# Top-k attention and a highway layer on one core: score tiles kept for the whole run, last rows' first products tied to one top-eight, and fewer unread products behind a layer's

## The chip, the cores and the metric

The kernel runs on one core of a Trainium2 chip. The metric is the device time in microseconds (us) of one execution; the time before is the median of three runs. The engines are named as the profile names them: PE is TensorE (PEld its weight loads), DVE is VectorE, ACT is ScalarE, POOL is GpSimd, SP is SyncE, which issues most of the DMAs.

## The reference

Eight batch elements, eight heads, 576 rows, head size 64. Each row of the scores keeps its 32 largest values; the rest is masked before the softmax. The heads' outputs of a row are joined to 512 features, and a highway layer follows.

```python
scores = scale * np.matmul(q, k.transpose(0, 1, 3, 2))          # (8, 8, 576, 576)
kth = np.partition(scores, -top_k, axis=-1)[..., -top_k:-top_k + 1]   # top_k = 32
scores = np.where(scores >= kth, scores, -1000000000.0)
attn = softmax(scores)                                          # exp(s - max), over its sum
x = np.matmul(attn, v), heads side by side                      # (4608, 512)
H = np.maximum(x @ w_h, 0.0)
T = 1.0 / (1.0 + np.exp(-(x @ w_t + b_t)))
out = T * H + (1.0 - T) * x
```

## The kernel before

**Items.** A unit is 128 query rows of one head, or, for the last 64 rows (576 = 4 x 128 + 64), the last rows of two heads one above the other. Two units make a pair, here called an item; `pairs` has 144, 18 for each batch element: 16 of full rows and, at the end, 2 of last rows. The scores of an item fill three banks of PSUM (512 columns each): unit 0 in bank 0 and the first 64 columns of bank 1, unit 1 in the last 64 columns of bank 1 and all of bank 2. Two such score tiles exist (pool `xps`, `bufs=2`), so the scores of item g can be written only when all is done with those of item g - 2.

**The top 32 of a row** are not sorted out in full. VectorE takes the top eight of each of six 96-column segments (`segments`, L358, twelve a step), and from these 48 `refine` finds the row's largest value and a threshold near rank 24 (L375 to L391). ScalarE turns the scores into a mask of what lies above the threshold and counts it (`mask_count`, L406, twice a step). TensorE adds the mask, at a large negative weight, onto the scores in PSUM (`mask_add`, L419), and VectorE takes the top eight of what is left in each unit's full row (`below`, L432, twice a step). From the count and these eight the 32nd value is picked (L438, L448, L451). Exponents (L424), a mask by the 32nd value (L454, L457) and their minimum (L471, L474) make the weights, which SP's transposing DMA turns (L496) for the product with v (L509, three steps later). ScalarE copies finished outputs out of PSUM (L523).

**The order.** The program is written out by hand: `step(i)` issues, for every engine, what belongs to items i + 2 (scores), i + 1 (segments, threshold, mask), i (mask products, full top-eight, exponents), i - 1 (weights) and i - 3 (product with v). Each engine runs its own list in this order; semaphores join them. On TensorE a step is: the mask products of item i (L419), the products with v of item i - 3 (L509), eight unread products (`spare`, L279; three where the items coming are of last rows and the output tile is begun anew), at times a piece of the preparation for the next batch element (transposes of q and k, L251 and L258), the scores of item i + 2, then a piece of preparation or a layer's products if there is one (L537 to L551), and again unread products: four behind such a piece, ten where there is none.

```python
        if i + 2 < NG:
            start_scores(i + 2)
        if layers and (last_steps or i <= SPB or kind[0] or not to_prep):
            ...
            late.append(layers.pop(0)())
        ...
        spare(4 if late else 10)
```

`spare(n)` issues n products of 252 columns into columns of the output tile that nobody reads. The scores of full-row items are L311 and L322, those of last rows L328 (two heads one after the other, four products each) and L339 (the last 64 columns). The layer's inputs are turned by another DMA (L602), and its products wait for it. `finish` handles the last item and the last blocks.

Of the kernel before, what the change touches and what calls it, by code (L numbers as in the profile page):

```python
# [11 lines left out]
FP32 = mybir.dt.float32  # L12
# [14 lines left out]
def kernel(  # L27
# [10 lines left out]
    nc = tc.nc  # L38
    P = nc.NUM_PARTITIONS
# [13 lines left out]
    BANK = 512  # L53
# [13 lines left out]
    pairs = [(u, u + 1) for u in range(0, NU, 2)]  # L67
# [10 lines left out]
    xpool = ctx.enter_context(tc.tile_pool(name="x", bufs=3))  # L78
    fpool = ctx.enter_context(tc.tile_pool(name="f", bufs=2))
    hpool = ctx.enter_context(tc.tile_pool(name="h", bufs=3))  # L80
    xps = ctx.enter_context(tc.tile_pool(name="xps", bufs=2, space=bass.MemoryType.PSUM))
    ops = ctx.enter_context(tc.tile_pool(name="ops", bufs=1, space=bass.MemoryType.PSUM))
    fps = ctx.enter_context(tc.tile_pool(name="fps", bufs=1, space=bass.MemoryType.PSUM))


    ident_f = consts.tile([P, P], FP32)
# [12 lines left out]
    TOP, THR, KTH = 0, 1, NPK + 1  # L99
    wall = consts.tile([P, NU + 2, NPK + 2], FP32)  # L100
# [174 lines left out]
    def spare(n):  # L275
        if "t" not in po:
            po.update(t=pso_tile(), n=0)
        for _ in range(n):
            nc.tensor.matmul(  # L279
                po["t"][:, 4 * DE : BANK],  # L280
                ident_b[:],
                cst[:, 0 : BANK - 4 * DE],
                start=True,
                stop=True,
                skip_group_check=True,
            )

    def prep_alloc(kd):
        kT = kqpool.tile([P, NP, MAIN], FP32, name="kT")
        qT = kqpool.tile([P, NP, S], FP32, name="qT")  # L290
        return kT, qT, kd
# [2 lines left out]

    def scores(pair, prep):
        kT, qT, kd = prep
        ps = xps.tile([P, 3 * BANK], FP32, tag="x", name="xs")
        heads2 = [units[u][2] for u in pair]  # L300
        qt = units[pair[0]][1]
        qs = qt * P
        MB = 2 * BANK
        rest = []
        RA, RB = BANK, 2 * BANK - rem
        if qt < nfull:
            hp = heads2[0][0] // 2
            for n0 in range(0, MAIN, 256):
                for s, mo in ((0, 0), (1, MB)):
                    r = s * D  # L310
                    mm = nc.tensor.matmul(  # L311
                        ps[:, mo + n0 : mo + n0 + 256],
                        qT[r : r + D, hp, qs : qs + P],
                        kT[r : r + D, hp, n0 : n0 + 256],
                        start=(n0 == 0),
                        stop=True,
                        skip_group_check=True,
                    )
                    if s:
                        rest.append(mm)  # L320
            ends = ps[:, BANK:MB].rearrange("p (a n) -> p a n", n=rem)[:, 0 :: BANK // rem - 1, :]
            rest.append(nc.tensor.matmul(ends, qT[:, hp, qs : qs + P], kd[:, hp, :], start=True, stop=True))  # L322
        else:
            for (mo, ro), hh in zip(((0, RA), (MB, RB)), heads2):
                hp = hh[0] // 2
                for n0 in range(0, MAIN, 256):
                    for r in (0, D):
                        mm = nc.tensor.matmul(  # L328
                            ps[r : r + rem, mo + n0 : mo + n0 + 256],
                            qT[r : r + D, hp, qs : qs + rem],  # L330
                            kT[r : r + D, hp, n0 : n0 + 256],
                            start=(n0 == 0),
                            stop=True,
                            skip_group_check=True,
                        )
                        if mo:
                            rest.append(mm)
                for r in (0, D):
                    mm = nc.tensor.matmul(  # L339
                        ps[r : r + rem, ro : ro + rem],  # L340
                        qT[r : r + D, hp, qs : qs + rem],
                        kd[r : r + D, hp, r : r + rem],
                        start=(mo == 0),
                        stop=True,
                        skip_group_check=True,
                    )
                    rest.append(mm)
        both = bass.AP(tensor=ps.tensor, offset=ps[:].offset, ap=[ps[:].ap[0], [3 * BANK - S, 2], [1, S]])
        return ps[:, 0:S], ps[:, 3 * BANK - S : 3 * BANK], both, rest
# [49 lines left out]
    def biases(g):  # L399
        return nc.gpsimd.tensor_tensor(be[:, g], wall[:, 2 * g : 2 * g + 2, TOP : KTH + 1 : KTH - TOP], fac[:], ALU.mult)  # L400
# [22 lines left out]
    def expo(u, sc, e):  # L423
        nc.scalar.activation(e, sc, AF.Exp, bias=tb(u), scale=scale)  # L424
        return e
# [3 lines left out]
        return [t[:, s, :] for s in range(2)] + [t]  # L429

    def below(u, ps):
        nc.vector.max(wall[:, u, THR + 1 : KTH], ps)  # L432


    def hits(pair):
# [83 lines left out]
    def pso_tile():  # L519
        return ops.tile([P, BANK], FP32, tag="po", name="pso")  # L520
# [192 lines left out]
    preps = {0: prep_alloc(kds[0])}  # L713
# [4 lines left out]
    st = {}  # L718
# [4 lines left out]
    def ensure_prep(b, hp):  # L723
        for it in ((b, hp, 0), (b, hp, 1), (b, 0, 7), (b, 0, 8)):
            if it not in done:
                done.add(it)
                prep_piece(stages[b], preps[b], *it[1:])()
# [10 lines left out]
    def start_scores(g):  # L738
        b = units[pairs[g][0]][0]
        for u in pairs[g]:  # L740
            for h in units[u][2]:
                ensure_prep(b, h // 2)
        st[g] = dict(ps=scores(pairs[g], preps[b]), sc=[None, None], et=[None, None], e=[None, None])
        st[g]["seg"] = 0
        st[g]["cand"] = cands[g % len(cands)]

    def copy_both(g):
        st[g]["sc"] = copy_scores(st[g]["ps"][2])


    def segs(g, n):
        if g >= NG:
            return
        for c in range(st[g]["seg"], min(2 * NSEG, st[g]["seg"] + n)):
            s, k = divmod(c, NSEG)
            segments(st[g]["cand"][:, s], st[g]["ps"][s], k, k + 1, () if s else st[g]["ps"][3])
        st[g]["seg"] += n
# [24 lines left out]
    late = []  # L782
    kind = [False]

    def masks_of(g):
        pr = pairs[g]
        views = (st[g]["ps"][0], st[g]["sc"][1])
        st[g]["m"] = [mask_count(u, views[s]) for s, u in enumerate(pr)]

    def step(i):  # L790
# [5 lines left out]
        b, k_in = divmod(i, SPB)  # L796
# [15 lines left out]
        if live:  # L812
            pr = pairs[i]
# [18 lines left out]
        segs(i + 1, 2 * NSEG)  # L832
        if live:
            below(pr[0], st[i]["ps"][0])
            below(pr[1], st[i]["ps"][1])
        if live:
            st[i]["e"] = pair_tile("e")
            expo(pr[0], st[i]["sc"][0], st[i]["e"][0])
# [9 lines left out]
        elif i > SPB:  # L848
            kind[0] = True
            piece = prep_filler()  # L850
            if piece:
                late.append(piece)
        spare(4 if late else 10)
        if live:
            expo(pr[1], st[i]["sc"][1], st[i]["e"][1])
        ra = refine(i + 1, st[i + 1]["cand"]) if nxt else iter(())
# [53 lines left out]
    def begin():  # L910
        done.update((0, hp, part) for hp in range(NP) for part in range(2))
        done.update(((0, 0, 7), (0, 0, 8)))
        piece = partial(prep_piece, stages[0], preps[0])
        dve = nc.vector.tensor_copy
        spare(21)
        xa = xps.tile([P, 3 * BANK], FP32, tag="x", name="xs")
        ev0 = piece(0, 3)
        ev1 = piece(0, 5, xa, dve)
        ev2 = piece(0, 4, po["t"], dve)
        ev1()  # L920
        ev0()
        ev2()
        piece(0, 2, xa[:, BANK : 2 * BANK], dve)()
        po.clear()
        start_scores(0)
        piece(0, 6, pso_tile())()
        evs = [piece(1, 0), piece(1, 5, pso_tile())]
        for ev in evs:
            ev()
        segs(0, 2 * NSEG)  # L930
        copy_both(0)
        start_scores(1)
        for _ in refine(0, st[0]["cand"]):
            pass
        biases(0)
        evs = [piece(2, 0), piece(2, 5, pso_tile())]
        masks_of(0)
        for ev in evs:
            ev()
        rest = [(0, 3, 0), (0, 3, 1), (0, 1, 6), (0, 2, 6)]  # L940
        done.difference_update(rest)
        to_prep.extend(rest)
        vs = loads_v(0, vbs[0])
        todo_v.extend(vs[H:] + vs[0:H] + loads_w() + [load_bt])
# [20 lines left out]
    def finish():  # L965
        i = NG - 1
        pr, pu = pairs[i], pairs[i - 1]
# [39 lines left out]
        cur["e"] = pair_tile("e")  # L1007
        for s, u in enumerate(pr):
            expo(u, cur["sc"][s], cur["e"][s])
        x1 = xps.tile([P, 3 * BANK], FP32, tag="x", name="xs")  # L1010
        project(bank(x1, 1), z["qt"], z["xT"], wt, True)
        blk_gate(z, bank(x1, 1))
        n = values_of(i - 2, 2 * DE)
# [4 lines left out]
        old["et"] = transposes(pu[0])  # L1018
        nc.vector.tensor_tensor(hit[:], hit[:], wall[:, pr[0] : pr[1] + 1, THR:KTH], ALU.mult)
        pick_b(pr, hit)  # L1020
        x2 = xps.tile([P, 3 * BANK], FP32, tag="x", name="xs")
        cur["et"] = halves(et_tile())
        turned = None
        for s, home in enumerate((bank(x2, 1), bank(x1, 0))):
# [47 lines left out]
    with tc.If(fine < 1):  # L1072
        with tc.For_i(0, B, 1) as bi:
# [21 lines left out]
            prep = prep_alloc(kds[0])  # L1095
# [4 lines left out]
            for pr in pairs[0 : NG // B]:  # L1100
                scs = copy_scores(scores(pr, prep)[2])
                for s, u in enumerate(pr):
                    b, qt, heads = units[u]
                    if heads[0] == 0:
                        xs = xpool.tile([P, H * DE], FP32, name="xs")
                    sc = scs[s]
# [10 lines left out]
                    e = pair_tile("e")[s]  # L1117
# [45 lines left out]
```

## Time and profile before

| what | value |
|---|---|
| median of 3 runs | 797.43 us (797.13 to 797.91) |
| the profiled execution | 797.43 us, its span 795.7 us |
| VectorE busy | 767.3 us (96%) |
| ScalarE busy | 756.3 us (95%) |
| TensorE busy | 693.0 us (87%) |
| GpSimd busy | 564.8 us (71%) |
| granted TensorE clock, mean | 0.996 |

The span is the time from the first instruction to the last in the profiled execution. A row of the groups by line names line, engine, operation and tiles, then the count, the busy time, the mean of one in ns, and the idle time of the engine just before them with what ended it. A row of the timeline has start and length in us and, in brackets, idle time before it. A row of the list of waits has the total, the number of waits and the longest. In a row of busy time by stretch the engines stand in the order PE, PEld, DVE, ACT, POOL, behind them the granted clock, the share of the DMA engines and GB/s.

### The profile page before, as it was taken

What the parts mean: (1) busy time and instruction counts of PE and PEld (TensorE: products, weight loads), DVE (VectorE), ACT (ScalarE), POOL (GpSimd) and SP (SyncE); (2) the same over time, 40 slices, a digit from 0 to 9 for tenths busy, and PEclk for the clock granted to TensorE, in tenths of its full rate; (3) what the DMA queues carried; (4) which work ended last, traced back from release to release, by engine and by line L of the source; (5) the groups of instructions that cost most, each with busy time, mean ns of one, the idle gap of its engine ahead of it and who ended that gap; (6) DMA issues with size and microseconds to landing.
All of it is one profiled execution on the core that took longest, in us unless ns stands there. A gap on an engine that the chain in (4) does not pass through costs nothing.

```text
span 795.7 us, 20350 instructions
## 1 busy us (share of the span) xinstructions
PE 693.0 (87%) x6459; PEld 494.6 (62%) x6459; DVE 767.3 (96%) x3947; ACT 756.3 (95%) x1401; POOL 564.8 (71%) x750
## 2 busy tenths in 40 slices
PE   8889988888988888888997889888998888988884
PEld 6666766566656666566665666656666666666552
DVE  6999999999999999999999999999999999999996
ACT  5999999999999999999999999999999999999984
POOL 2666867877778767787777876788777787776760
PEclk9999999999999999999999999999999999999998
DMA  6699967976899567987689866898677975565643
GB/s 125 88 136 172 127 125 140 159 127 87 140 157 156 104 99 135 159 136 117 106 146 159 133 110 111 154 154 127 107 129 146 162 118 96 97 113 98 114 85 89
DMA packets 341780, 100.32 MB, mean 126 GB/s; under 512 B 326048, under 2 KB 333856, under 8 KB 341664
## 3 DMA queue, kind: packets, MB, share of 16 engines
q1 hardware_dynamic: 286448, 79.14, 52.6%
q0 software_dynamic: 53536, 19.34, 22.5%
q8 instruction: 53, 0.87, 0.4%
q10 hardware_dynamic: 1680, 0.46, 0.3%
q14 instruction: 63, 0.52, 0.2%
HBM read 31.72 MB, written 9.44 MB: 52 GB/s over the span
## 4 chain that ended last, share of the span: by engine, by line
DVE 46%; ACT 32%; PE 16%; issue 2%; DMA 2%; SPq 0%; POOL 0%; DVEq 0%; ACTq 0%; POOLq 0%
DVE cand L358 16%; DVE wall L432 15%; ACT m L406 9%; ACT e L424 8%; ACT sc L353 6%; DVE ep L471 6%; ACT r L454 4%; PE xs L328 4%; PE fp L537 3%; PE pso L279 3%; PE xs L419 2%; PE xs L311 2%; DMA xT<-xb 2%; ACT xs L523 2%; DVE en L382 1%
## 5 line engine op out<-in xcount | busy, mean ns | idle before, releaser
L358 DVE MAX8 cand<-xs 128x8 f32<-128x96 f32 x1728 | 298.0, 252 | 0.4 <-PE xs L311 0.2
L279 PE MATMUL pso<-cst,ident_b 128*128 128x252 bf16 x1841 | 247.1, 272 | 41.8 <-ACT xs L523 39.7
L457 POOL TENSOR_SCALAR r<-sc,wall 128x576 bf16<-128x576 f32 x135 | 232.5, 1722 | 0.0
L424 ACT ACTIVATE e<-sc,be 128x576 bf16<-128x576 f32 x288 | 227.8, 791 | 0.1
L279 PEld LDWEIGHTS <-ident_b 128*128 128x128 bf16 x1841 | 173.5, 98 | 80.7 <-issue 48.9
L432 DVE MAX8 wall<-xs 128x8 f32<-128x576 f32 x288 | 205.2, 756 | 13.3 <-PE xs L419 12.1
L311 PE MATMUL xs<-kT,qT 64*128 64x256 f32 x1024 | 145.3, 400 | 34.0 <-DVE high L375 26.0
L353 ACT COPY sc<-xs 128x1152 f32<-128x1152 f32 x144 | 161.7, 1123 | 0.2
L311 PEld LDWEIGHTS xs<-kT,qT 64*128 64x128 f32 x1024 | 93.0, 186 | 65.5 <-issue 39.3
L406 ACT ACTIVATE m<-xs,wall 128x576 int8<-128x576 f32 x144 | 108.1, 751 | 9.8 <-DVE wall L391 8.6
L471 DVE TENSOR_TENSOR ep<-e,r 128x1024 bf16<-128x1024 bf16 (+2 forms) x236 | 116.4, 493 | 0.3 <-issue 0.2
L448 POOL TENSOR_TENSOR hit<-hit,wall 128x18 f32<-128x18 f32 x143 | 32.1, 225 | 113.5 <-DVE hit L438 113.5
L419 PE MATMUL xs<-m,ident_b 128*128 128x512 bf16 (+1 forms) x576 | 104.7, 285 | 9.0 <-ACT m L406 6.8
L406 ACT ACTIVATE m<-sc,wall 128x576 int8<-128x576 f32 x144 | 112.5, 781 | 0.0
L454 ACT ACTIVATE r<-sc,be 128x576 bf16<-128x576 f32 x143 | 111.0, 776 | 0.0
L509 PEld LDWEIGHTS <-et 128*128 128x128 bf16 (+1 forms) x1600 | 68.6, 100 | 19.9 <-issue 3.5
L400 POOL TENSOR_TENSOR be<-wall,fac 128x4 f32<-128x4 f32 x144 | 29.0, 201 | 71.9 <-DVE ep L471 52.0
L509 PE MATMUL pso<-vb,et 128*128 128x65 bf16 (+1 forms) x1600 | 74.4, 194 | 1.0 <-DMA et<-ep 1.0
L419 PEld LDWEIGHTS <-ident_b 128*128 128x128 bf16 x576 | 51.1, 98 | 35.5 <-issue 13.9
L322 PEld LDWEIGHTS xs<-kd,qT 128*128 128x128 f32 x256 | 38.1, 188 | 42.5 <-issue 42.1
L322 PE MATMUL xs<-kd,qT 128*128 128x128 f32 x256 | 62.5, 326 | 0.0
L625 POOL TENSOR_TENSOR s<-h,x 128x512 f32<-128x512 f32 (+1 forms) x37 | 42.8, 1157 | 1.0 <-ACT h L624 1.0
(128 smaller groups left out, 1005.8 us busy)
## 6 DMA issues: line engine op xcount, KB each, us to landing
kin<-in_k_dram SPq DMA_DIRECT2D x64, 128.0 KB, 3.2
qin<-in_q_dram SPq DMA_DIRECT2D x62, 128.0 KB, 3.1
out_dram<-s SPq DMA_DIRECT2D x30, 256.0 KB, 3.1
s<-h POOLq DMA_DIRECT2D x29, 256.0 KB, 3.8
xb<-x POOLq DMA_DIRECT2D x30, 128.0 KB, 2.7
vb<-in_v_dram POOLq DMA_DIRECT2D x28, 128.0 KB, 3.9
et<-ep SPq DMA_TRANSPOSE x143, 3.9
vb<-in_v_dram POOLq DMA_DIRECT2D x24, 64.0 KB, 3.0
```

The costliest lines, as they stand in the source:

```text
L279: nc.tensor.matmul(po["t"][:, 4 * DE : BANK], ident_b[:], cst[:, 0 : BANK - 4 * DE], start=True, stop=True, skip_group_check=True,)
L311: mm = nc.tensor.matmul(ps[:, mo + n0 : mo + n0 + 256], qT[r : r + D, hp, qs : qs + P], kT[r : r + D, hp, n0 : n0 + 256], start=(n0 == 0), ...
L353: nc.scalar.copy(sc[:], both)
L358: ins = nc.vector.max(cand[:, s, :], sc[:, s * SEG : (s + 1) * SEG])
L406: nc.scalar.activation(m1[:].bitcast(I8)[:, 1 : 2 * S : 2], ps, AF.Sign, bias=wall[:, u, THR : THR + 1], scale=ABOVE, accum_out=csum[:, u ...
L419: nc.tensor.matmul(ps[:, s0:s1], ident_b[:], m1[:, s0:s1], start=False, stop=True, skip_group_check=True)
L424: nc.scalar.activation(e, sc, AF.Exp, bias=tb(u), scale=scale)
L432: nc.vector.max(wall[:, u, THR + 1 : KTH], ps)
L454: nc.scalar.activation(r, sc, AF.Relu, bias=eb(u), scale=BIGK)
L457: nc.gpsimd.tensor_scalar(r, sc, kth(u), None, ALU.is_ge)
L471: return nc.vector.tensor_tensor(out[:, :, c0:c1], e[:, :, c0:c1], r[:, :, c0:c1], ALU.min)
L509: nc.tensor.matmul(pso[r0 : r0 + ql, col : col + DE], ets[s][:, c, gi * P2 : gi * P2 + ql], vb[:, h, vc, :], start=(c == 0), stop=(c == nc ...
```

## The change

Three edits go together. First, the two score tiles are made once and kept for the run (`xss`), item g using tile g % 2; before, each item took a new tile from a pool of two. Second, the first four products of a last-row item (the ones into bank 0) are declared independent of the second full top-eight (unit 1's) of item g - 2, so that they wait for that item's first full top-eight only; `below` returns its instruction for this. Third, `spare(4 if late else 10)` becomes `spare(1 if late else 10)`: one unread product, not four, behind a layer's products or a piece of preparation. In the changed program's order of instructions there are 1481 unread products where there were 1841; the first L339 product of 16 last-row items has a wait on VectorE that it had not; and the first score product of 80 items no longer waits for TensorE's own signal beside another engine's.

```diff
-    xps = ctx.enter_context(tc.tile_pool(name="xps", bufs=2, space=bass.MemoryType.PSUM))
+    xps = ctx.enter_context(tc.tile_pool(name="xps", bufs=1, space=bass.MemoryType.PSUM))
...
+    xss = [xps.tile([P, 3 * BANK], FP32, name=f"xs{i}") for i in range(2)]
...
-    def scores(pair, prep):
+    def scores(pair, prep, other=None):
+        def ahead(mm):
+            if other is not None:
+                tc.declare_no_dep(mm.ins, other.ins, reason="another bank")
+
         kT, qT, kd = prep
-        ps = xps.tile([P, 3 * BANK], FP32, tag="x", name="xs")
+        ps = xss[pair[0] // 2 % 2]
...
                         if mo:
                             rest.append(mm)
+                        else:
+                            ahead(mm)
...
     def below(u, ps):
-        nc.vector.max(wall[:, u, THR + 1 : KTH], ps)
+        return nc.vector.max(wall[:, u, THR + 1 : KTH], ps)
...
-        st[g] = dict(ps=scores(pairs[g], preps[b]), sc=[None, None], et=[None, None], e=[None, None])
+        st[g] = dict(ps=scores(pairs[g], preps[b], st[g - 2]["below"] if g > 1 else None), sc=[None, None], et=[None, None], e=[None, None])
...
             below(pr[0], st[i]["ps"][0])
-            below(pr[1], st[i]["ps"][1])
+            st[i]["below"] = below(pr[1], st[i]["ps"][1])
...
-        spare(4 if late else 10)
+        spare(1 if late else 10)
...
-        xa = xps.tile([P, 3 * BANK], FP32, tag="x", name="xs")
+        xa = xss[1]
...
-        x1 = xps.tile([P, 3 * BANK], FP32, tag="x", name="xs")
+        x1 = xss[i % 2 ^ 1]
...
-        x2 = xps.tile([P, 3 * BANK], FP32, tag="x", name="xs")
+        x2 = xss[i % 2]
```

## The prediction

> **What bounds the kernel now.** I read the page first, for who is busy and what ends the waits of the busiest engine.
>
> ```profile
> PE 693.0 (87%) x6459; PEld 494.6 (62%) x6459; DVE 767.3 (96%) x3947; ACT 756.3 (95%) x1401; POOL 564.8 (71%) x750
> L279 PE MATMUL pso<-cst,ident_b 128*128 128x252 bf16 x1841 | 247.1, 272 | 41.8 <-ACT xs L523 39.7
> L432 DVE MAX8 wall<-xs 128x8 f32<-128x576 f32 x288 | 205.2, 756 | 13.3 <-PE xs L419 12.1
> ```
>
> VectorE is busy 767.3 of 795.7 us, ScalarE 756.3. Of VectorE's 28.4 idle us, 13.3 lie before one line, the full top-eight (L432), and there it waits for TensorE's mask products (L419). That is the most that a faster TensorE can give. The list of waits says how the 12.1 are spread, and what makes TensorE late; the busy times of one batch element (18 steps) say how much room stands behind it.
>
> ```profile
> DVE wall L432 <- PE xs L419: 12.1, 25, 1.1
> PE fp L537 <- DMA xT<-xb: 2.6, 3, 1.1
> ACT m L406 <- DVE wall L391: 8.6, 23, 0.9
> 483.10:578.29 95.19, 83.95 (x791) 59.55 (x788) 94.12 (x488) 93.77 (x174) 72.14 (x95) 1.00 0.77 131
> ```
>
> In this batch element VectorE idles 95.19 - 94.12 = 1.07 us, ScalarE 1.42. So VectorE sets the pace, ScalarE stands 0.35 us behind it over 18 steps, and TensorE (third column) only delays VectorE at certain steps. Which steps: grouping by line in the stretches that hold the two last-row items of a batch element gives, for eight stretches, one row of 0.7, six like the second here, and one of 1.4 (the last).
>
> ```profile
> L432 DVE MAX8 wall<-xs 128x8 f32<-128x576 f32 x2 | 1.4, 758 | 0.7 <-PE xs L419 0.7
> L432 DVE MAX8 wall<-xs 128x8 f32<-128x576 f32 x4 | 2.9, 758 | 1.1 <-PE xs L419 1.1
> L432 DVE MAX8 wall<-xs 128x8 f32<-128x576 f32 x4 | 2.9, 758 | 1.4 <-PE xs L419 0.7 <-PE pso L509 0.7
> ```
>
> 0.7 + 6 x 1.1 + 1.4 = 8.7 of the 13.3 us belong to the last-row items. One such pair in order of time, TensorE first, then VectorE, then ScalarE:
>
> ```profile
> 472.09 0.48 PE L279 MATMUL pso<-cst,ident_b 128*128 128x252 bf16 x3 [0.70 <-ACT xs L523]
> 472.97 1.08 PE L328 MATMUL xs<-kT,qT 64*64 64x256 f32 x8 [0.40 <-DVE wall L432]
> ...
> 475.95 0.59 PE L279 MATMUL pso<-cst,ident_b 128*128 128x252 bf16 x4
> 476.38 0.65 PE L419 MATMUL xs<-m,ident_b 128*128 128x512 bf16 x4
> 477.19 1.02 PE L279 MATMUL pso<-cst,ident_b 128*128 128x252 bf16 x8
> 478.04 0.60 PE L251 MATMUL fp<-ident_f,qin 128*128 128x128 f32 x4
> 478.72 1.08 PE L328 MATMUL xs<-kT,qT 64*64 64x256 f32 x8
> 479.60 0.31 PE L339 MATMUL xs<-kd,qT 64*64 64x64 f32 x4
> ...
> 481.91 0.59 PE L279 MATMUL pso<-cst,ident_b 128*128 128x252 bf16 x4
> 482.34 0.65 PE L419 MATMUL xs<-m,ident_b 128*128 128x512 bf16 x4
> 471.50 1.41 DVE L432 MAX8 wall<-xs 128x8 f32<-128x576 f32 x2
> 477.14 1.43 DVE L432 MAX8 wall<-xs 128x8 f32<-128x576 f32 x2 [0.35 <-PE xs L419]
> 480.31 2.07 DVE L358 MAX8 cand<-xs 128x8 f32<-128x96 f32 x12
> 483.10 1.43 DVE L432 MAX8 wall<-xs 128x8 f32<-128x576 f32 x2 [0.72 <-PE xs L419]
> 488.25 1.42 DVE L432 MAX8 wall<-xs 128x8 f32<-128x576 f32 x2
> 479.84 0.73 ACT L406 ACTIVATE m<-xs,wall 128x576 int8<-128x576 f32 x1
> 480.56 0.76 ACT L406 ACTIVATE m<-sc,wall 128x576 int8<-128x576 f32 x1
> 483.35 0.38 ACT L523 COPY xs<-pso 128x260 f32<-128x260 f32 x1 [0.64 <-PE pso L509]
> 485.97 0.74 ACT L406 ACTIVATE m<-xs,wall 128x576 int8<-128x576 f32 x1
> 486.69 0.78 ACT L406 ACTIVATE m<-sc,wall 128x576 int8<-128x576 f32 x1
> ```
>
> The mask was ready at 481.32 (480.56 + 0.76), but TensorE reached its mask products only at 482.34: it had started the next item's last-row scores when the second full top-eight ended (477.14 + 1.43 = 478.57), then did the scores, a layer's products and four unread products. The path from that top-eight through TensorE to the next one ends last here, nowhere else for long.
>
> **The change part by part.** *One unread product for four.* Eight take 1.02 us, of which the last's own 0.27: (1.02 - 0.27) / 7 = 0.107 us each. The changed program has 1481 of them where there were 1841: 120 steps lose three, 0.32 us each. They stand straight before the mask products, so where TensorE is late the mask products come 0.32 us sooner; where the mask is late TensorE only waits longer, and the cost and the gain are nothing.
>
> *Early last-row products.* The first four products of a last-row item (the 0.88 us from 478.72 to 479.60) now wait for the first top-eight of the item two back, which ends 1.43 / 2 = about 0.7 us before the second; the last-column products behind them (L339) still wait for the second. That is a wait added at a new place: behind it on TensorE stand the other half of the scores, the layer's products and the mask products that VectorE needs. It costs nothing as long as the four take longer, 0.88, than the second top-eight, 0.7. This happens 16 times. In the first step of the pair TensorE was free at 472.09 + 3 x 0.107 = 472.41 and began at 472.97: 0.55 us gained. In the second it was free at about 478.48 (four prep products from 478.04, 0.109 apart), but everything ahead of that moves up with the earlier mask products, so the limit is the first top-eight, and the gain the whole 0.7. Full-row items keep the wait for both (their first product waits once, for the later one), so the kept tiles in themselves bring them nothing; the wait on TensorE's own signal that goes there stood beside a longer one, and I price it at nothing. No instruction is added, nor moved on the queues of SP or POOL.
>
> The first step of the pair is shortened on TensorE by 0.32 + 0.55 = 0.87 against a wait of 0.35, the second by 0.32 + 0.7 = 1.0 against 0.72. Both waits go: 1.07 us in this pair. What is late next is ScalarE. Where ScalarE bounds, the top-eight begins 0.65 us after the second mask ends:
>
> ```profile
> 316.55 0.78 ACT L406 ACTIVATE m<-sc,wall 128x576 int8<-128x576 f32 x1
> 317.98 1.43 DVE L432 MAX8 wall<-xs 128x8 f32<-128x576 f32 x2 [0.15 <-PE xs L419]
> ```
>
> (317.98 - 317.33). In the second step that is 481.32 + 0.65 = 481.97, and VectorE itself is ready at 480.31 + 2.07 - 0.35 = 482.03: nothing given back yet. One step on, ScalarE's work from mask to mask is 485.97 - 479.84 less the idle 0.64 = 5.49, so the mask starts at 485.33, ends 486.69 + 0.78 - 485.97 = 1.50 later at 486.83, and the top-eight can begin at 487.48; VectorE would be there at 488.25 - 1.07 = 487.18. So 0.30 of the 1.07 is given back and a pair brings 0.77. Six such are 4.6; the two other stretches (0.7 and 1.4) at the same share, 0.77 / 1.07 = 0.72, are 1.5: **6.1 us**.
>
> *The other waits.* Three of them come from a layer's products that wait for a transposing DMA, the longest like this:
>
> ```profile
> 433.17 1.04 PE L537 MATMUL fp<-wh,xT 128*128 128x512 bf16 x4 [1.14 <-DMA xT<-xb]
> 435.24 1.43 DVE L432 MAX8 wall<-xs 128x8 f32<-128x576 f32 x2 [1.09 <-PE xs L419]
> ```
>
> The transfer stays where it is; only the three unread products behind it go: 3 x 0.32 = **1.0**. The remaining 13.3 - 8.7 less these three (about 2.3) is 2.3 us in a dozen small waits: I give **0.8** of it, since in about half of them the mask itself is late, as at 317.98, and ScalarE stays. Sum 6.1 + 1.0 + 0.8 = 7.9. The profiled execution took 797.43 us, 1.7 more than its span and the same as the median of the runs: 797.4 - 7.9 = **789.5**.
>
> Bounds of the sum: below, half of it if ScalarE (0.35 us behind per 18 steps) gives back most of what follows each pair, 4 us; above, all waits on TensorE gone but those behind the DMA, 11 us.
>
> **The clock.** The unread products also keep TensorE busy. At the start 21 of them took 0.22 us each; later 0.107: by that the clock ran at half there, though the granted clock of this stretch doesn't mark it.
>
> ```profile
> 1.83 4.59 PE pso L279 x21
> 777.00:788.00 11.00, 8.31 (x104) 5.34 (x102) 9.28 (x20) 7.54 (x17) 0.00 (x0) 1.00 0.36 103
> 778.00:781.40 3.40, 2.10 (x42) 1.65 (x39) 3.16 (x7) 3.31 (x7) 0.00 (x0) 1.00 0.50 96
> ```
>
> Towards the end TensorE was busy 76% of 11 us, and 62% of the thinnest 3.4 us in it, and the granted clock stayed 1.00. The change takes at most 0.32 of some 5.3 us a step, 6 points of a hundred, so the batch element above goes from 88% to some 84% at worst in its mean (15 such steps, 4.8 us of 95.2 off, against 0.8 us off its length). That lies well above what the trace shows as safe, and I take no cost. [...]
>
> **The rivals.** *The clock falls* (0.08). TensorE's work of a step is 83.95 / 18 = 4.7 us, 4.4 without the three; at half clock 8.8, so a step of 5.3 becomes 8.8 and loses 3.5. It decides from 7.9 / 3.5, between two and three steps at half clock in the whole run; with one in each of the eight batch elements it is 8 x 3.5 - 7.9 = 20 slower, 817. For it: nothing but the thinner work; against it: the rows above.
> *ScalarE takes the place of TensorE* (0.22). It is 0.35 us behind per batch element, and its 8.6 us of waits for VectorE (L391) are not all to be had, as it cannot work ahead. Then half of the gain stays, 4 us: 793.4.
> *Only the unread products tell* (0.08): the early products meet a TensorE that is not free, or wait as before. A pair then brings 0.32 + 0.32 = 0.64, at the share of 0.72 it is 0.46; with 0.32 and 2 x 0.32 from the odd stretches 6 x 0.46 + 0.7 = 3.5, and 1.8 from the rest: 5.3, 792.1.
> *ScalarE gives nothing back* (0.12): the waits of pairs go whole and most small ones too, 8.7 + 1.0 + 1.3 = 11.0: 786.4.
>
> **How the numbers follow.** Forecast 0.50, the rivals 0.08, 0.22, 0.08 and 0.12. A measurement of this kernel can tell about 0.2%, 1.6 us, from no change. Faster by more holds all but the clock's case and a remainder of ScalarE's: 0.87; within 0.2%: 0.04; slower: 0.09. The range leaves out the clock's case; it runs from the gain of 11 to that of 4, and a microsecond beyond each for the small waits, of which I split only the sum: 785.4 to 794.4.
>
> **What would show it.** Right: L432's idle falls from 13.3 to about 5 us, with what is left before it behind late masks or the DMA; L279 counts 1481; the first of the L328 groups starts some 0.6 us earlier against its step; ScalarE's wait of 0.64 at L523 goes; the granted clock stays at 1.00 in all middle stretches. Wrong: clock below 1.00 between 15 and 770 us; L432's idle above 9; or a longer mean of L358 or L432, which nothing here lets me expect.

## The result, and the profile after

| | median of the runs | profiled execution | its span |
|---|---|---|---|
| before | 797.63 us (4 runs, 797.13 to 797.91) | 797.43 us | 795.7 us |
| changed | 787.99 us (4 runs, 786.82 to 788.33) | 787.68 us | 786.0 us |

The ratio is 0.9875 (95% interval 0.9861 to 0.9889). The medians differ by 9.6 us, where 7.9 were forecast (789.5), inside the range. Line numbers are 7 higher in the changed kernel, 1 higher for the unread products: the full top-eight is L439, its mask products L426, the mask L413, the segments' top-eights L365, the last-row scores L333 and L346, the unread products L280. The page of the changed kernel, first the engines, then the two groups shown of before:

```profile
PE 660.2 (84%) x6020; PEld 454.9 (58%) x6099; DVE 765.8 (97%) x3947; ACT 752.7 (96%) x1401; POOL 565.3 (72%) x750
L280 PE MATMUL pso<-cst,ident_b 128*128 128x252 bf16 x1481 | 207.6, 272 | 45.7 <-ACT xs L530 43.3
L439 DVE MAX8 wall<-xs 128x8 f32<-128x576 f32 x288 | 203.9, 748 | 3.9 <-ACT h L631 1.2
```

The idle time before the full top-eight fell from 13.3 to 3.9 us, 9.4 of the 9.7 us by which the span is shorter. VectorE's own work is the same 3947 instructions, but its busy time fell by 1.5 us too; that belongs to the same closed waits, as is shown below. Against it stand 1.2 us of new idle time at other places: VectorE idled 795.7 - 767.3 - 13.3 = 15.1 us outside this line before, 786.0 - 765.8 - 3.9 = 16.3 after.

The list of waits, then the batch element shown of before:

```profile
PE xs L426 <- ACT m L413: 21.8, 65, 0.5
PE fp L544 <- DMA xT<-xb: 4.0, 5, 1.1
DVE wall L439 <- ACT h L631: 1.2, 4, 0.6
DVE wall L439 <- PE xs L426: 0.9, 4, 0.3
476.57:571.08 94.51, 79.52 (x728) 53.82 (x734) 94.06 (x488) 93.24 (x176) 72.26 (x95) 1.00 0.81 133
```

VectorE waited 25 times and 12.1 us for mask products; now 4 times and 0.9 us. It is TensorE that now waits for the mask, 65 times and 21.8 us, where it was 26 times and 6.8 us before. In the batch element VectorE idles 94.51 - 94.06 = 0.45 us, where it was 1.07; the granted clock stays 1.00. The pair of last-row items whose rows the prediction shows, in the changed kernel, VectorE first, then TensorE, then ScalarE:

```profile
466.14 1.41 DVE L439 MAX8 wall<-xs 128x8 f32<-128x576 f32 x2
471.35 1.41 DVE L439 MAX8 wall<-xs 128x8 f32<-128x576 f32 x2
474.50 2.07 DVE L365 MAX8 cand<-xs 128x8 f32<-128x96 f32 x12
476.57 1.43 DVE L439 MAX8 wall<-xs 128x8 f32<-128x576 f32 x2
481.79 1.43 DVE L439 MAX8 wall<-xs 128x8 f32<-128x576 f32 x2
...
467.15 1.08 PE L333 MATMUL xs<-kT,qT 64*64 64x256 f32 x8
470.13 0.27 PE L280 MATMUL pso<-cst,ident_b 128*128 128x252 bf16 x1
470.24 0.73 PE L426 MATMUL xs<-m,ident_b 128*128 128x512 bf16 x4
472.51 1.08 PE L333 MATMUL xs<-kT,qT 64*64 64x256 f32 x8
475.81 0.65 PE L426 MATMUL xs<-m,ident_b 128*128 128x512 bf16 x4
...
474.36 0.77 ACT L413 ACTIVATE m<-xs,wall 128x576 int8<-128x576 f32 x1
475.08 0.81 ACT L413 ACTIVATE m<-sc,wall 128x576 int8<-128x576 f32 x1
476.98 0.41 ACT L530 COPY xs<-pso 128x260 f32<-128x260 f32 x1
479.59 0.79 ACT L413 ACTIVATE m<-xs,wall 128x576 int8<-128x576 f32 x1
```

Both bracketed waits at the full top-eight are gone, and ScalarE's wait of 0.64 at its copy (L530) too. One unread product (470.13) stands where four stood, and the mask products behind it begin 1.1 us ahead of the top-eight that needs them. The first group of last-row scores starts 467.15 - 466.14 = 1.01 us into its step, before 472.97 - 471.50 = 1.47: 0.46 us earlier, where the prediction named some 0.6. From the top-eight at 466.14 to the one at 476.57 the two steps take 10.43 us; before, from 471.50 to 483.10, 11.60. Measured from start to start like this, the pair gained 1.17 us, and all eight pairs together 8.7 (0.8 to 1.6 each). This length of two steps is what the experiments are compared by; it does not depend on when a DMA lands elsewhere.

### The profile page after: what moved, and what is told of

The parts are those of the page before. It is cut to its first block, busy times and chain, and to the rows that moved or that the text cites. A ratio compares the mean times of both kernels' runs of the same rounds, so it can differ in the third digit from the quotient of the medians.

```text
span 786.0 us, 19482 instructions
## 1 busy us (share of the span) xinstructions
PE 660.2 (84%) x6020; PEld 454.9 (58%) x6099; DVE 765.8 (97%) x3947; ACT 752.7 (96%) x1401; POOL 565.3 (72%) x750
## 4 chain that ended last, share of the span: by engine, by line
ACT 47%; DVE 40%; PE 6%; DMA 3%; issue 2%; SPq 1%; another core or an unknown queue 0%; DVEq 0%
DVE cand L365 15%; ACT m L413 13%; ACT e L431 12%; DVE wall L439 11%; ACT sc L360 10%; DVE ep L478 6%; ACT r L461 6%; DMA xT<-xb 2%; ACT xs L530 2%; ACT kT L253 1%; DVE en L389 1%; DVE en L392 1%; ACT h L631 1%; DMA et<-ep 1%; ACT qT L253 1%
## 5 line engine op out<-in xcount | busy, mean ns | idle before, releaser
L365 DVE MAX8 cand<-xs 128x8 f32<-128x96 f32 x1728 | 297.5, 246 | 0.5 <-PE xs L316 0.2
L280 PE MATMUL pso<-cst,ident_b 128*128 128x252 bf16 x1481 | 207.6, 272 | 45.7 <-ACT xs L530 43.3
L431 ACT ACTIVATE e<-sc,be 128x576 bf16<-128x576 f32 x288 | 232.1, 806 | 0.1
L439 DVE MAX8 wall<-xs 128x8 f32<-128x576 f32 x288 | 203.9, 748 | 3.9 <-ACT h L631 1.2
L280 PEld LDWEIGHTS <-ident_b 128*128 128x128 bf16 x1481 | 140.1, 98 | 74.3 <-issue 52.5
L360 ACT COPY sc<-xs 128x1152 f32<-128x1152 f32 x144 | 163.7, 1137 | 0.1
L316 PEld LDWEIGHTS xs<-kT,qT 64*128 64x128 f32 x1024 | 88.3, 186 | 66.6 <-DVE wall L439 49.4
L426 PE MATMUL xs<-m,ident_b 128*128 128x64 bf16 (+1 forms) x523 | 100.5, 275 | 25.9 <-ACT m L413 21.8
L413 ACT ACTIVATE m<-xs,wall 128x576 int8<-128x576 f32 x144 | 109.9, 763 | 8.9 <-DVE wall L398 8.1
L413 ACT ACTIVATE m<-sc,wall 128x576 int8<-128x576 f32 x144 | 114.4, 794 | 0.0
L461 ACT ACTIVATE r<-sc,be 128x576 bf16<-128x576 f32 x143 | 112.8, 789 | 0.0
L426 PEld LDWEIGHTS <-ident_b 128*128 128x128 bf16 x576 | 54.3, 97 | 69.3 <-issue 40.8
L633 POOL TENSOR_TENSOR h<-h,x 128x512 f32<-128x512 f32 (+1 forms) x37 | 43.0, 1162 | 1.3 <-DVE ep L481 0.8
```

What stands on the lines that cost most here:

```text
L280: nc.tensor.matmul(po["t"][:, 4 * DE : BANK], ident_b[:], cst[:, 0 : BANK - 4 * DE], start=True, stop=True, skip_group_check=True,)
L316: mm = nc.tensor.matmul(ps[:, mo + n0 : mo + n0 + 256], qT[r : r + D, hp, qs : qs + P], kT[r : r + D, hp, n0 : n0 + 256], start=(n0 == 0), ...
L360: nc.scalar.copy(sc[:], both)
L365: ins = nc.vector.max(cand[:, s, :], sc[:, s * SEG : (s + 1) * SEG])
L413: nc.scalar.activation(m1[:].bitcast(I8)[:, 1 : 2 * S : 2], ps, AF.Sign, bias=wall[:, u, THR : THR + 1], scale=ABOVE, accum_out=csum[:, u ...
L426: nc.tensor.matmul(ps[:, s0:s1], ident_b[:], m1[:, s0:s1], start=False, stop=True, skip_group_check=True)
```

## The experiments

| kernel | this pair, us | all eight pairs, us less than before | ratio to before, 95% interval | us faster than before, by the ratio |
|---|---|---|---|---|
| before | 11.60 | | | |
| fewer unread products alone | 10.96 | 4.9 | 0.9922 (0.9908 to 0.9936) | 6.2 |
| kept tiles and early products alone | 10.99 | 4.3 | 0.9950 (0.9938 to 0.9963) | 4.0 |
| kept tiles alone | 11.52 | 1.0 | 0.9997 (0.9987 to 1.0007) | 0.2 |
| all three: the change | 10.43 | 8.7 | 0.9875 (0.9861 to 0.9889) | 10.0 |

The lengths of the pairs come from one profiled execution of each kernel, the ratios from all its runs. In this section "us faster" goes by the ratio, which is not exactly that of the medians: for the change it gives 10.0 us, the medians 9.6.

**Fewer unread products alone.** The kernel before with

```diff
-        spare(4 if late else 10)
+        spare(1 if late else 10)
```

> The kernel before with only the third edit: one unread product for four. Theory of the sum, as on record: a pair of last-row items keeps 0.40 of its 1.07 us of waits, the DMA waits and the small ones shrink as with the whole change; 5.3 us faster than before, by the shares on record. The same theory with what the changed kernel's trace adds (ScalarE gave back 0.07 a pair and not 0.30; the small and the DMA waits brought more than 1.8): 6 to 7 us faster. If only the unread products tell, the whole gain of the change is here: 9.6 us. If thinner work lowers the clock: slower, and a granted clock under 1.00 in the middle.

Measured: 0.9922, 6.2 us faster than before, as the sum had it with what the changed kernel's trace adds (6 to 7), more than by the shares on record (5.3). The pair keeps a wait of 0.40 in its second step, as worked out:

```profile
467.48 1.41 DVE L432 MAX8 wall<-xs 128x8 f32<-128x576 f32 x2
472.79 1.43 DVE L432 MAX8 wall<-xs 128x8 f32<-128x576 f32 x2
478.44 0.77 DVE L432 MAX8 wall<-xs 128x8 f32<-128x576 f32 x1 [0.40 <-PE xs L419]
```

0.72 - 0.32 = 0.40: the size of the term was right to a hundredth.

**Kept tiles and early products alone.** The changed kernel with `spare(4 if late else 10)`.

> The changed kernel with four unread products again: kept tiles and early last-row products alone. Theory of the sum: the first step of a pair is shortened by 0.55 against a wait of 0.35, the second by about 0.7 against 0.72, so both waits nearly go in each of the eight pairs and nothing else does: 7 to 8 us faster than before, with the DMA waits as before. If only the unread products tell: within 1 us of before. If ScalarE takes TensorE's place: about 4 us faster.

Measured: 0.9950, 4.0 us faster: a miss, and the 4 us of the case in which ScalarE takes TensorE's place. But it is not ScalarE that holds the pair up. The first step's wait went, the second kept 0.56 of 0.72:

```profile
470.26 1.41 DVE L439 MAX8 wall<-xs 128x8 f32<-128x576 f32 x2
475.47 1.41 DVE L439 MAX8 wall<-xs 128x8 f32<-128x576 f32 x2
481.25 0.77 DVE L439 MAX8 wall<-xs 128x8 f32<-128x576 f32 x1 [0.56 <-ACT tt L655]
474.67 0.65 PE L426 MATMUL xs<-m,ident_b 128*128 128x512 bf16 x4
475.16 0.48 PE L516 MATMUL pso<-vb,et 128*128 128x65 bf16 x10
475.47 1.02 PE L280 MATMUL pso<-cst,ident_b 128*128 128x252 bf16 x8
476.33 0.60 PE L252 MATMUL fp<-ident_f,qin 128*128 128x128 f32 x4
476.86 1.08 PE L333 MATMUL xs<-kT,qT 64*64 64x256 f32 x8
480.49 0.65 PE L426 MATMUL xs<-m,ident_b 128*128 128x512 bf16 x4
```

(The bracket names ScalarE; what ended last is the mask products of 480.49, which run to 481.14. ScalarE's mask for them was ready at 479.19 + 0.81 = 480.00, and TensorE was still at its scores, a layer's products and four unread products.) The first top-eight ended at 475.47 + 0.7 = 476.2, but TensorE was at work without a break until the prep piece was done, and began the scores at 476.86, hardly before the second top-eight ended (476.88). From the mask products to the scores TensorE has 2.2 us of its own work, whatever VectorE does.

**Five unread products ahead of the scores, with the early products.** The kernel just shown with

```diff
-        spare(8 if i + 2 >= NG or units[pairs[i + 2][0]][1] < nfull or po["n"] else 3)
+        spare(5 if i + 2 >= NG or units[pairs[i + 2][0]][1] < nfull or po["n"] else 3)
```

> Kept tiles and early products, four unread products behind a layer's, and five in place of eight ahead of the scores. In the run with the early products alone the second step of a pair kept a wait of 0.56: TensorE reached the scores only when its eight unread products and the prep piece were done, and not when the first top-eight was. If that is the limit, three fewer ahead of the scores bring the scores 0.32 sooner, the 0.56 becomes 0.24, and the whole is 2 to 2.6 us faster than early products alone: about 6 to 6.6 faster than before. If the top-eight is the limit, as the prediction had it, or ScalarE: the same as early products alone, 4 us faster than before.

Measured: 0.9882 (0.9868 to 0.9897), 9.4 us faster than before, more than either theory had. In the pair it is as the first had it: the wait went from 0.56 to 0.25 and two steps take 479.18 - 468.51 = 10.67.

```profile
468.51 1.41 DVE L439 MAX8 wall<-xs 128x8 f32<-128x576 f32 x2
479.18 0.77 DVE L439 MAX8 wall<-xs 128x8 f32<-128x576 f32 x1 [0.25 <-PE xs L426]
```

Eight pairs at 0.32 are 2.6 of the 5.4 us between the two kernels. The rest lies in other steps. In the profile of the kernel before this one TensorE waited for the layer's turning DMA 6.6 us (7 times), in this one 2.1 us (3 times), and most of the steps outside the pairs in which the two profiles differ by over 0.4 us hold such a wait in one of them; whether that goes for all runs is not shown.

**The same five, without the early products.** The edit just shown on the kernel before.

> The kernel before with five in place of eight unread products ahead of the scores, and nothing else. With early products this brought 5.4 us (from 4.0 to 9.4 faster than before). Theory that TensorE's own work ahead of the scores and the wait for the second full top-eight end at the same time in the kernel before: without early products TensorE only waits longer for the top-eight, so 0 to 0.7 us faster than before. Rival: the unread products hold TensorE up wherever they stand, and the early products need not be there: 4 us or more faster than before.

Measured: 0.9979 (0.9970 to 0.9989), 1.7 us faster: more than the 0 to 0.7 expected, far from the rival's 4, and nothing of it in the pairs: two steps take 481.07 - 469.48 = 11.59. Where the 1.7 come from stays open. In the pair the time that TensorE has free brings nothing without the early products, 0.32 us with them.

```profile
469.48 1.41 DVE L432 MAX8 wall<-xs 128x8 f32<-128x576 f32 x2
481.07 0.77 DVE L432 MAX8 wall<-xs 128x8 f32<-128x576 f32 x1 [0.73 <-PE xs L419]
```

**Kept tiles alone.** The changed kernel with `spare(4 if late else 10)` and `None` in place of `st[g - 2]["below"]`.

> The kernel before with only the tiles kept; the first last-row products wait for both full top-eights as before, four unread products as before. Theory of the sum: no change, within 0.5 us. Rival: the tiles taken from a pool cost something themselves (a second wait at 80 products); then 1 us or more faster.

Measured: 0.9997, no difference to within a microsecond. The pair's waits are nearly as before, 0.63 in place of 0.72 in the second step:

```profile
472.80 1.41 DVE L439 MAX8 wall<-xs 128x8 f32<-128x576 f32 x2
484.32 0.77 DVE L439 MAX8 wall<-xs 128x8 f32<-128x576 f32 x1 [0.63 <-PE xs L426]
```

**A lighter ScalarE, on the changed kernel and on the one before.**

```diff
-            expo(pr[0], st[i]["sc"][0], st[i]["e"][0])
+            expo(pr[0], st[i]["sc"][0][:, 64:S], st[i]["e"][0][:, 64:S])
...
-            expo(pr[1], st[i]["sc"][1], st[i]["e"][1])
+            expo(pr[1], st[i]["sc"][1][:, 64:S], st[i]["e"][1][:, 64:S])
```

and three kept tiles for the exponents, set to zero once. This kernel leaves out the weights of 64 of the 576 keys; it is there to measure what ScalarE's time is worth.

> The changed kernel with ScalarE's two exponents of a step cut by 64 of 576 columns (weights of 64 keys of each unit are left at zero, in kept tiles): 0.13 us less of ScalarE a step, nothing else less. If ScalarE takes back what the pairs gain (0.14 us a pair, and the small waits behind a late mask): 1 to 2 us faster than the changed kernel. If ScalarE doesn't bind: the same. If it had taken half, as that rival had it: 4 us faster.

> The kernel before with the same cut of ScalarE's exponents (64 of 576 columns of both units left at zero). With the change this brought 3.7 us, by the traces 1.0 of it in the pairs and 2.9 in other steps, where a late mask held up VectorE before the change too. So 2 to 3 us faster than before here. If ScalarE binds only once TensorE's waits are gone: within 0.7 us of before. If ScalarE is worth the same in both: 3.7 us.

(The 0.13 us is an estimate. By ScalarE's copies before, 383 ns for 260 columns and 1123 for 1152, 128 columns would be 0.11.)

Measured: 0.9828 (0.9815 to 0.9840) on the changed kernel, which against its own 0.9875 is 0.0047 of the time before, 3.7 us; and 0.9982 (0.9973 to 0.9991), 1.4 us, on the kernel before. The first expectation was too low and the second too high: a lighter ScalarE is worth more than twice as much once TensorE's waits are gone, so some 2.3 us of what TensorE gave up went to ScalarE. About 0.8 of them lie in the eight pairs, which a lighter ScalarE shortens by 1.0 us on the changed kernel and by 0.2 on the one before. The three intervals leave the 2.3 uncertain by more than a microsecond.

**None behind a layer's products, then none in the steps at all.** `spare(0 if late else 10)`, and for the second kernel `spare(0)` at both places.

> The changed kernel with none in place of one unread product behind a layer's products. Theory of the sum: 0.107 us sooner only where TensorE is still late (about 8 steps, most behind a DMA): 0.3 to 0.8 us faster than the changed kernel, about 10 faster than before. If the clock is near its edge: granted clock under 1.00 in the middle, and slower than the changed kernel.

> The changed kernel without any unread product in the steps (those at the start and in the last item stay). Theory that the clock is not near its edge: granted clock 1.00 in the middle though TensorE is busy under 70%; TensorE is never late but behind a DMA, so 0.5 to 1.5 us faster than the changed kernel, about 10.5 to 11 faster than before. The clock's rival: granted clock well under 1.00 in many stretches and slower than the changed kernel, by 3.5 us for each step at half clock.

Measured: 0.9873 (0.9855 to 0.9890) with none behind, the same as the change; and 1.0265 (1.0231 to 1.0299) with none at all, 21 us slower than before. There the clock fell. The second kernel's row of the engines, the page's rows of the granted clock, and six stretches of the second kernel:

```profile
PE 573.1 (70%) x4645; PEld 359.4 (44%) x4645; DVE 768.9 (95%) x3947; ACT 756.4 (93%) x1401; POOL 564.9 (69%) x750
PEclk9999999999999999999999999999999999999998
...
PEclk9778899899898998889997999979998699969998
21.70:31.90 10.20, 8.14 (x35) 4.94 (x35) 8.69 (x51) 9.03 (x18) 7.03 (x10) 0.50 0.59 62
31.90:38.70 6.80, 3.42 (x38) 2.17 (x35) 6.80 (x32) 6.18 (x12) 3.90 (x6) 1.00 0.74 94
35.31:38.72 3.41, 1.13 (x14) 0.67 (x13) 3.41 (x15) 3.27 (x8) 2.40 (x3) 1.00 1.03 98
38.70:42.10 3.40, 3.24 (x14) 2.08 (x15) 3.06 (x21) 3.40 (x7) 2.87 (x5) 0.50 1.00 141
42.10:49.00 6.90, 3.34 (x37) 2.06 (x34) 6.90 (x35) 5.91 (x12) 3.71 (x5) 0.99 0.97 141
49.00:55.80 6.80, 5.89 (x32) 3.97 (x34) 6.53 (x37) 6.64 (x12) 4.24 (x7) 0.50 0.90 162
```

The first PEclk row is the changed kernel's, the second that of the kernel with none. TensorE is busy 3.42 of 6.80 us at full clock, and only 1.13 of the last 3.41 of them; then the clock is halved for 3.4 us, TensorE is busy nearly throughout (3.24 of 3.40), VectorE loses 0.34, and the clock comes back. The other two halved rows are 10.2 and 6.8 us long. The mean granted clock of this execution was 0.895, which, with all that is lost put down to 0.50, makes (1 - 0.895) x 813.1 x 2 = 171 us at half clock; the changed kernel's 0.996 of 786.0 us makes 6, so 165 us are new.

**Early products for full-row items too.** Unit 0's two products first and marked `ahead(mm)`, then unit 1's.

> The changed kernel with the early products for full-row items too: unit 0's two products first, independent of the second full top-eight, then unit 1's two. Theory of the sum: in full-row steps TensorE is late only behind a DMA, so nothing is gained, within 0.7 us of the changed kernel. Rival (TensorE's wait for the top-eight, 28.5 us in the changed kernel, holds up the pace): 2 us or more faster than the changed kernel.

Measured: 0.9878 (0.9863 to 0.9893), no difference to the change. Its profile is of use for another reason: compared by the starts of the same steps' top-eights, it falls behind the changed kernel's at two places, by 1.5 and 1.3 us, and at each the clock was halved once, from 142.7 and from 333.9. The first with the 3.41 us ahead of it and the 3.4 behind it, then the second with the stretch ahead of it:

```profile
139.31:142.72 3.41, 2.13 (x21) 1.34 (x22) 3.41 (x16) 3.37 (x10) 3.30 (x4) 1.00 0.79 135
142.70:146.10 3.40, 3.32 (x16) 2.21 (x15) 2.44 (x14) 3.40 (x7) 2.70 (x6) 0.50 1.26 134
146.10:149.50 3.40, 3.40 (x34) 2.16 (x30) 2.92 (x14) 2.64 (x6) 2.26 (x2) 0.99 1.18 161
330.50:333.90 3.40, 1.85 (x22) 1.20 (x21) 3.40 (x15) 3.37 (x9) 2.71 (x4) 1.00 1.25 169
333.90:337.30 3.40, 3.40 (x16) 2.07 (x14) 2.30 (x16) 3.40 (x8) 2.34 (x5) 0.50 0.83 166
```

Behind 3.4 us with TensorE 54% busy VectorE loses 3.40 - 2.30 = 1.1 us in the next 3.4. The first fall came behind a stretch that was 62% busy; from there VectorE idles 3.40 - 2.44 = 0.96 and 3.40 - 2.92 = 0.48 us in two rows.

**One behind and five ahead**, the two edits together on the changed kernel.

> The changed kernel with five in place of eight unread products ahead of the scores: one behind, five ahead. TensorE is no longer late in the pairs, so by the sum nothing more is gained but 0.3 us behind the DMA: within 0.7 us of the changed kernel as long as the clock holds. [...]

Measured: 0.9897 (0.9877 to 0.9917), not faster than the change; its six runs spread from 787.92 us at a mean granted clock of 0.997 to 793.28 at 0.990 and 792.23 at 0.988. Its profile, the one at 0.988, has the clock at 0.50 for 10.2 us, from 119.5 to 129.7, so the clock did not hold in all of its runs.

**The layer's turning DMA one step earlier**, `turns.append((i + 1, ...))` for `(i + 2, ...)`.

> The changed kernel with the DMA that turns a layer's input issued one step earlier. TensorE still waited 4.0 us, five times, for this DMA, and VectorE 1.2 us behind it. If the transfer only starts late: these waits go, 1 to 2 us faster than the changed kernel. Rival: the DMA before it (the cast to bf16) hasn't landed by then, SP's queue stands still behind the turn, and the turns of the weights behind it come late: 1 us or more slower than the changed kernel.

Measured: 0.9934 (0.9921 to 0.9946), 4.7 us slower than the change. TensorE's waits for this DMA grew:

```profile
PE fp L544 <- DMA xT<-xb: 8.4, 6, 2.0
```

from 4.0 to 8.4 us. By the program the layer's products move up together with the DMA's issue; why they wait longer is not shown, nor whether the rival's reason, SP's queue standing still, holds. Not all of the loss need be the DMA's: in this profile, the slowest of the five runs (796.04 us, the others 792.09 to 793.31), the mean granted clock was also lower, 0.990 where the others have 0.994 and 0.995.

No kernel that does all the work beat the change by more than the intervals.

## Why the prediction was right, and by what it was off

**What bounds the kernel: right.** VectorE sets the pace, TensorE was late at known steps, and those waits went, from 13.3 to 3.9 us (forecast: to about 5). The pairs brought 2.6 us more than their term, and all else about 1.0 (9.7 - 8.7) where 1.8 was forecast, so in the sum a part of the error cancels.

**The unread products: right in size.** 0.32 us a step; the run with them alone shows 0.40 left of 0.72.

**The early products: right in the first step, wrong in the second.** The prediction let the first top-eight be the limit there and gave 0.7 us. Alone they brought 0.16 (0.72 - 0.56), because TensorE itself was not free. In the whole change this did no harm: the first step is shortened on TensorE by more than its wait (0.32 + 0.46 = 0.78 by the rows, 0.87 by the prediction, against 0.35), TensorE carries the surplus into the second, and 0.32 of unread products are left out there too. The two parts add up in the pair: 0.64 + 0.61 = 1.25, against 1.17 with both.

**The pairs: the term that was mis-sized**, 6.1 us forecast and 8.7 measured. Two parts of the working were off, and both come from one way of reading rows. An idle time in brackets is counted from the end of the instruction before. But instructions that follow each other without a wait can overlap, here by 0.09 us. In the profile of before, one step behind the pair:

```profile
486.27 2.07 DVE L358 MAX8 cand<-xs 128x8 f32<-128x96 f32 x12
488.25 1.42 DVE L432 MAX8 wall<-xs 128x8 f32<-128x576 f32 x2
```

The top-eight starts at 488.25, 0.09 us before the segments' end at 488.34. A bracket of 0.35 is therefore a delay of 0.44, and one of 0.72 is 0.81. This is how the pair's first step came from 477.14 - 471.50 = 5.64 to 471.35 - 466.14 = 5.21 us, 0.43 less. For about fifteen closed waits it makes 1.4 us, and it is why VectorE's busy time, which counts an overlap once, fell by 1.5. ScalarE's work from mask to mask was overrated by the same error: with 0.64 idle taken off it came out as 5.49 us; the changed kernel shows 479.59 - 474.36 = 5.23. From start to start, the copy in question began 1.24 us behind the activation ahead of it (483.35 - 482.11), in the changed kernel 0.48 (476.98 - 476.50), so it was late by 0.76; and that activation itself was late by 0.13, without a bracket. 485.97 - 479.84 less these two is 5.24. So ScalarE gave back 0.07 in the step after the pair (481.79 - 476.57 = 5.22, before 488.25 - 483.10 = 5.15) and not 0.30.

**The waits behind the DMA: cannot be sized from one execution.** TensorE waited for the turning DMA 2.6 us (3 times) in the profile of before, 4.0 (5 times) after, 3.4 with fewer unread products alone and 6.6 with the early products alone, though none of these kernels changes how that DMA is issued. The forecast of 1.0 is neither shown nor refuted.

**ScalarE in TensorE's place: partly so.** That rival gave it half of the gain. The runs with a lighter ScalarE put what it took at some 2.3 us, though less of it in the pairs than the prediction had.

**The clock: right that it would not matter here, wrong in the reason.** "Well above what the trace shows as safe" compared means. The falls above came behind single thin stretches of 3.4 us, 33%, 54% and 62% busy. With four unread products behind a layer's too, the mean granted clock was 0.994 in the profile with the kept tiles alone, against 0.996 in that of before; by 0.002 x 2 x 798.9 that is some 3 us more at half clock. But no share of its own decides: the changed kernel has stretches as thin as the last two, 55% and 58% here, and stays at full clock behind both:

```profile
762.65:766.06 3.41, 1.87 (x23) 1.53 (x24) 2.79 (x5) 2.16 (x7) 1.47 (x2) 1.00 0.38 74
370.11:373.52 3.41, 1.99 (x23) 1.16 (x22) 3.41 (x16) 3.41 (x9) 2.60 (x3) 1.00 1.03 119
```

So the forecast that the clock would hold came true with less room than it claimed, and in part by luck. The price in the rival was too high as well: 3.5 us a step by the prediction, where 165 us more at half clock, 31 steps' worth, cost some 27 (814.8 us in that profiled execution, 787.7 in the changed kernel's). In the changed kernel's four runs the order of the times is that of the mean granted clock (786.82 us at 0.997, 787.68 at 0.996, 788.30 at 0.995, 788.33 at 0.994); four runs are too few to show that the one follows from the other.

## What to carry to other kernels

A wait in brackets understates the delay where instructions otherwise overlap, by 0.09 us here: measure a step from start to start, with and without the wait. When two edits shorten one chain at two places, the surplus of the first is spent at the second, so cost the chain and not each place against its own wait. Work that only keeps a clock up can be cut where the chain is late, as long as the clock holds. Here it fell behind single stretches of 3.4 us that were 33%, 54% and 62% busy and held behind two of 55% and 58%, so how thin they may become had to be measured.

## What the runs showed of the hardware

In the rows by stretch above, the granted clock of TensorE is 1.00 or, for 3.4, 6.8 or 10.2 us at a time, 0.50; 0.99 stands where a row takes in a little of both. Ahead of three of these falls TensorE was busy 33%, 54% and 62% of 3.4 us. In the profiles of the kernel before and of the changed one the clock is 1.00 from 17.67 and 15.13 us up to the last item and falls there, at 789.08 and at 779.71 us, behind 3.4 us with TensorE 38% busy (1.31 of 3.42) and 26% (0.90 of 3.41). Counted back from this fall in stretches of 3.41 us, the changed kernel has five of 220 (15.13 to 766.06 us) that are under 65% busy, from 55% to 64%, and the kernel before one of 220 (17.67 to 768.60 us), at 62%; the clock stayed at 1.00 behind all six. So 54% and 62% were followed by a fall and 55% to 64% were not; why is open. (Busy time is modelled, and some matmuls may lack a record, so the shares are rough.)

A fall of 3.4 us cost 1.3 to 1.5 us in the two cases compared, with 1.44 us of VectorE idle in two rows behind the first and 1.10 in one behind the second. The 165 us more of the kernel without unread products in its steps cost it some 27, 0.6 for each 3.4, so most of them must lie where TensorE has time to spare; that is worked out from the sum and not shown one by one.
